# Causal attention on one core: half blocks of keys in 64 by 64 tiles, with loads and routing steps in other places

## The chip, the cores and the metric

The kernel runs on one core of one Trainium2 chip. A core has five engines with a queue each: TensorE (PE; its weight loads are listed apart as PEld) multiplies matrices into PSUM, VectorE (DVE), ScalarE (ACT) and GpSimd (POOL) work element by element, SyncE (SP) only starts transfers here. The metric is the device time of one execution in microseconds; less is better. Before the change the median of three runs is 746.33 us (744.14 to 746.45).

## The reference

Two layers follow each other. The first is a causal attention with a bias that lowers the weight of keys by what was summed up between key and query:

```python
scores = scale * np.matmul(q, k.transpose(0, 1, 3, 2))          # B, H, S, D = 8, 8, 576, 64
cum = np.cumsum(np.maximum(s, 0.0), axis=-1)
bias = -(cum[:, :, :, None] - cum[:, :, None, :])
scores = np.where(causal, -1e9, scores + np.minimum(bias, 0.0))
attn = exp(scores - max) / (sum + 1e-9)
x = matmul(attn, v)                                             # then (B, S, 512)
```

The second routes each of the 4608 tokens of 512 numbers to one of 8 experts, by the largest of 8 logits or, where a local gate says so, by the choice of the token ahead of it. Its output is `p[e] * (relu(x @ w1[e]) @ w2[e])` with 1024 hidden numbers. All is in float32.

## The kernel before, in words

**Work.** There are 32 pairs of heads (n = 0 to 31, `NPAIR`; 4 pairs make a batch). The two heads of a pair lie on partitions 0 to 63 and 64 to 127 of `qb` and `kb`. Scores are made with keys on the output's partitions: `scores(n, u)` (L893) makes one of four units of `UNITS` (L40), each up to 448 query columns wide, into a PSUM tile `ps` of two banks, one for each head. ACT takes the exponential into an SBUF tile `e` (L905), and POOL sets what lies above the diagonal to zero (`masked`, L889). A unit has blocks of 128 keys, and each block is multiplied by all queries from its first one on. Since a step of queries is 64 wide, half of the first 64 by 128 columns of a block is work for nothing. The bias is not added to the scores: it factors into a weight of the key, exp(cum minus a reference), that is multiplied into v (`weigh`, L876, into `vg`), and two columns beside v carry the weight and a one, so that the products hold the sums too.

`values(n, j0, j1)` (L924) forms the outputs of query blocks j of 64: 128 keys by 64 queries of `e` are the stationary operand, 66 columns of `vg` the moving one, and the results of the blocks add up in `po`. The blocks 0 to 5 have one PSUM bank (`po0`), the blocks 6 to 8 another (`po6`), and both are used by all pairs in turn. `evacuate` (L938) divides on DVE by the sum (a reciprocal and a product) and puts the result into `xb`. `turn` (L947) transposes it for the routing products.

**Order.** All engines run in the order in which the program is written (a schedule by hand). The loop at L1002 has 16 slots m, each with two pairs: the scores of both, then the values of both, then transposes and the weighing of later pairs (`WEIGHED`). Between these stand places, `at(m, 0)` to `at(m, 5)`, at which steps of routing and of the experts are put in (`plan`, L964): 0 and 1 behind the scores of the first and second pair, 3 and 4 behind the values of the first and second pair, 5 at the slot's end. A step's instructions stand on each engine in this order. A group of two batches is routed in steps: `product` (TensorE), `logits`, `codes`, `turn1`, `exps` (ACT), `turn2`, `ranks` (TensorE), `rows`, `gates` (mostly DVE), and then 18 `scatter` steps of POOL, which write rows of `xb` to a table in DRAM, placed by `STORES` (L49). In place 3, 4 and 5 a scatter first copies a number of `recs`, the reciprocal of the last values, so POOL waits there for DVE. `assign_early` (L411) chooses the experts of the first units; the expert stage (`Experts.run`, L649) then runs over units of up to 256 tokens.

**Loads.** SP starts them in order. `load_qk` (L790) and `load_v` (L802) take a buffer that an earlier pair has left; with `behind`, ACT first copies one number into the buffer, from a tile that is made at a chosen point, and this holds the load back until that point. In each slot, two v tiles go behind the second pair's unit 1, and the four tiles of q and k for the slot after the next behind the values of the first pair. PSUM has eight banks: `ps_s` holds three tiles of two banks that units, routing products and other short products use in turn (`banks`, L784), and `ps_o` the two of `po`.

## Time and profile before

| what | time |
|---|---|
| median of three runs | 746.33 us |
| the profiled execution | 748.85 us |
| its span, from the first instruction to the last | 747.1 us |
| attention, slots 1 to 15 (start of the first scores to the first expert product) | 19.85 to 221.63 us |
| TensorE busy | 729.2 us |
| exponentials of the scores on ACT, 128 of them | 97.0 us |
| masks on POOL, 160 of them | 67.2 us |
| scatters of rows to the table on POOL, 54 counted together | 54.5 us |

Times are of one profiled execution. "Busy" counts a stretch in which an instruction of the engine runs; matmuls overlap in a pipeline, so the mean time of one is not the pace at which they follow each other. A group's line gives source line, engine, operation, output and inputs, shapes and count, then busy time, mean time in ns, and the idle time ahead of it with what ended it. In the chain that ended last each piece is what the next one waited for; "issue" stands for time in which nothing that is recorded was waited for.

### The profile page before, as it was taken

Reading aid. Unit: us, or ns where it says so; the run is one execution under the profiler, and the core shown is the slowest. Engines: PE = TensorE matmul, PEld = TensorE weight load, DVE = VectorE, ACT = ScalarE, POOL = GpSimd, SP = SyncE. Lnnn points to the kernel's source line nnn. Section 1 sums busy time; section 2 is a strip of 40 time slices with the busy share of each in tenths; the row PEclk is TensorE's granted clock in tenths of the full one; section 3 lists DMA queues with packets and bytes.
Section 4 is the critical chain, followed back from the end, with each engine's and each line's share of the span. In section 5 each row is a group of like instructions: output and inputs, shape, how many; then the busy total and the mean of one; then the engine's idle time right before and its main releaser. Section 6 shows DMA issues by size and latency. Waiting matters only on the chain.

```text
span 747.1 us, 16231 instructions
## 1 busy us (share of the span) xinstructions
PE 729.2 (98%) x6537; PEld 504.9 (68%) x6537; DVE 257.7 (34%) x714; ACT 166.0 (22%) x355; POOL 206.7 (28%) x453
## 2 busy tenths in 40 slices
PE   8999999999998999999999999999999999999996
PEld 7888878878876567567567365637644676673675
DVE  4656668677756383101100411041132001104110
ACT  4645454354331011011011010201010111110111
POOL 3543367577574245350100011010101001000100
PEclk9999999999998999999999999999999999999999
DMA  8464455665629996598555979996999965976700
GB/s 303 145 189 149 152 191 165 201 199 172 188 81 382 341 396 218 208 424 240 203 190 169 375 258 396 342 382 237 425 334 390 423 215 214 307 268 239 269 15 32
DMA packets 57205, 187.28 MB, mean 251 GB/s; under 512 B 11837, under 2 KB 32061, under 8 KB 49568
## 3 DMA queue, kind: packets, MB, share of 16 engines
q1 hardware_dynamic: 50224, 165.91, 62.3%
q0 software_dynamic: 6800, 20.09, 7.0%
q8 instruction: 53, 0.87, 0.5%
q14 instruction: 32, 0.26, 0.1%
q10 hardware_dynamic: 96, 0.15, 0.1%
HBM read 165.50 MB, written 20.75 MB: 249 GB/s over the span
## 4 chain that ended last, share of the span: by engine, by line
PE 95%; issue 2%; POOL 1%; DVE 1%; DMA 1%; ACT 0%; SPq 0%; POOLq 0%; ACTq 0%
PE yp L637 34%; PE hp L608 31%; PE po L934 13%; PE ps L904 11%; PE hp L599 4%; PE lp L217 2%; DMA qb<-in_q_dram 1%; POOL table L349 0%; ACT e L905 0%; PE pos L301 0%; POOL e L890 0%; PE pos L302 0%; DVE xb L942 0%; SPq L799 0%; POOL out_dram L641 0%
## 5 line engine op out<-in xcount | busy, mean ns | idle before, releaser
L637 PE MATMUL yp<-w2b,hT 128*128 128x512 f32 (+4 forms) x768 | 258.4, 584 | 0.0
L608 PE MATMUL hp<-xT,w1b 128*128 128x256 f32 (+2 forms) x1216 | 232.0, 352 | 0.0
L608 PEld LDWEIGHTS hp<-xT,w1b 128*128 128x128 f32 x1216 | 207.7, 192 | 30.0 <-issue 7.8
L637 PEld LDWEIGHTS yp<-w2b,hT 128*128 128x128 f32 (+3 forms) x768 | 109.9, 167 | 138.4 <-issue 136.1
L641 POOL DMA_INDIRECT out_dram<-y,gi x37 | 36.4, 984 | 412.3 <-DVE y L639 380.0
L610 ACT ACTIVATE hT<-hp 128x256 f32<-128x256 f32 (+2 forms) x152 | 53.6, 353 | 430.4 <-PE hp L608 417.2
L639 DVE TENSOR_SCALAR y<-yp,gi 128x512 f32<-128x512 f32 (+2 forms) x38 | 27.8, 731 | 299.8 <-PE yp L637 293.4
L934 PE MATMUL po<-vg,e 128*64 128x66 f32 x3200 | 105.2, 223 | 6.9 <-issue 5.6
L934 PEld LDWEIGHTS po<-vg,e 128*64 128x64 f32 x3200 | 98.7, 138 | 13.1 <-issue 10.5
L905 ACT ACTIVATE e<-ps 128x768 f32<-128x768 f32 (+1 forms) x128 | 97.0, 837 | 46.5 <-PE ps L904 45.8
L904 PE MATMUL ps<-qb,kb 64*128 64x192 f32 (+4 forms) x768 | 94.7, 398 | 0.6 <-ACT e L905 0.3
L904 PEld LDWEIGHTS ps<-qb,kb 64*128 64x128 f32 x768 | 64.7, 186 | 29.6 <-ACT e L905 14.9
L890 POOL TENSOR_SCALAR_AFFINE_SELECT e<-e 128x256 f32<-128x256 f32 (+1 forms) x160 | 67.2, 444 | 50.3 <-ACT e L905 49.3
L349 POOL DMA_INDIRECT table<-xb,idx x54 | 54.5, 1009 | 19.6 <-issue 16.8
L619 DVE STREAM_TRANSPOSE hT<-hs 32x256 f32<-32x256 f32 x64 | 27.9, 436 | 78.9 <-ACT hs L601 78.1
L884 DVE TENSOR_TENSOR vg<-va,wk 128x256 f32<-128x256 f32 x64 | 41.5, 714 | 0.0
L941 DVE RECIPROCAL recs<-po 128x12 f32<-128x12 f32 x64 | 13.5, 211 | 64.0 <-PE po L934 45.2
L599 PE MATMUL hp<-w1b,xT 128*32 128x512 f32 (+1 forms) x224 | 28.3, 594 | 0.0
L578 DVE STREAM_TRANSPOSE xT<-xq 128x1024 f32<-128x1024 f32 (+1 forms) x23 | 23.6, 1028 | 11.8 <-DMA xq<-table 11.7
L942 DVE TENSOR_TENSOR xb<-po,recs 128x384 f32<-128x384 f32 (+1 forms) x48 | 22.0, 458 | 2.2 <-POOL xb L325 0.6
L599 PEld LDWEIGHTS hp<-w1b,xT 128*32 128x32 f32 (+1 forms) x224 | 8.1, 114 | 17.8 <-issue 17.8
L953 DVE STREAM_TRANSPOSE xt<-xb 128x576 f32<-128x576 f32 x24 | 17.1, 751 | 0.0
(254 smaller groups left out, 202.6 us busy)
## 6 DMA issues: line engine op xcount, KB each, us to landing
w2b<-in_w_dram SPq DMA_DIRECT2D x30, 2048.0 KB
w1b<-in_w_dram SPq DMA_DIRECT2D x29, 2048.0 KB
va<-in_v_dram SPq DMA_DIRECT2D x32, 320.0 KB
kb<-in_k_dram SPq DMA_DIRECT2D x31, 288.0 KB
qb<-in_q_dram SPq DMA_DIRECT2D x31, 288.0 KB
xq<-table SPq DMA_DIRECT2D x56, 130.0 KB
w1b<-in_w_dram SPq DMA_DIRECT2D x4, 512.0 KB
xq<-table SPq DMA_DIRECT2D x20, 65.0 KB
```

The lines of the kernel that those rows point to most:

```text
L349: put = self.nc.gpsimd.indirect_dma_start(out=self.halves, in_=src, element_offset=0, in_offset=None, out_offset=bass.IndirectOffsetOnAxis ...
L599: mm(ps[d, :], lhsT=xT[:, k, d], rhs=self.ws[l][0][:, k, c * 512 : c * 512 + 512], start=(k == 0), stop=(k == DK - 1))
L608: mm(ps[:, :w], lhsT=self.ws[ls[0]][0][:, k, c * P : c * P + P], rhs=xT[:, k, :w], start=(k == 0), stop=(k == DK - 1))
L610: nc.scalar.activation(self.hT[u][:, c, :w], ps[:, :w], Act.Relu)
L619: self.nc.vector.transpose(hT[32 * a : 32 * a + 32, :, 32 * r : 32 * r + 32], hs[32 * r : 32 * r + 32].rearrange("p (c i) -> p c i", i=P)[ ...
L637: mm(ps[d, :], lhsT=hT[:, k, n * P + d.start : n * P + d.stop], rhs=self.ws[l][1][:, k, f : f + w], start=(k == 0), stop=(k == FK - 1))
L641: put = nc.gpsimd.indirect_dma_start(out=self.out[:, :], out_offset=bass.IndirectOffsetOnAxis(ap=gi.bitcast(I32)[:m, n, 0:1], axis=0), in_ ...
L884: nc.vector.tensor_tensor(vg[:, to].rearrange("p c h e -> p (c h) e")[:, :, :DH], va[:, :c].rearrange("p c h e -> p (c h) e"), wk[:, n, to ...
L890: nc.gpsimd.affine_select(out=ap, in_=ap, compare_op=Alu.is_ge, fill=0.0, base=base, pattern=n, channel_multiplier=-1)
L904: mm(ps[:, h, at : at + z - a], lhsT=kb[d, key : key + P], rhs=qb[d, a:z], start=True, stop=True)
L905: nc.scalar.activation(e, ps, Act.Exp, scale=scale)
L934: mm(po[d, j - j0, :], lhsT=weights_of(n, c, j, h), rhs=vgs[n % NV][:, c if j < 2 * G1 else G1 + c, h, :], start=(c == 0), stop=(c == last))
```

## The change

The keys of a pair are stored in another order of blocks of 64: 8, 0, 1, 2, 3, 5, 4, 7, 6 (`BLOCKS`). Blocks 0 and 1, 2 and 3, 5 and 4, 7 and 6 form the tiles of 128 keys, and block 8 stands alone. A tile now is multiplied only by the queries from its second block in time on. The products of the query blocks 0, 2, 4 and 6 with their own keys are left out there. They are made apart, by `scores_halves`, in products of 64 keys by 64 queries over 64 rows, for both pairs of a slot into one PSUM tile, with one exponential and two masks, and kept in `eh`. `values_halves` multiplies them by v, again 64 by 64. Scores have three units in place of four (widths 512, 448, 384), and the values of a pair 21 steps per head in place of 25, with four half ones.

The order within a slot becomes: scores of both pairs; values of the first pair and its halves; halves of the second pair; half scores of the next slot; the first pair's two divisions; place 3; the values of the second pair, each part with its division; place 4. The second pair's sums lie in a tile of `ps_s`, the first pair's in `ps_o`, and the blocks are split 0 to 3 and 4 to 8.

Loads go out in three parts: two v tiles behind the first pair's unit 2, q and k of one pair behind the second pair's unit 1, q and k of the other behind the second pair's unit 2. At the start four v tiles are loaded in place of six, q and k of pair 3 ahead of v of pair 2, and q and k of pair 0 in other pieces. `logits`, `turn2`, `rows`, `gates` and `assign_early` move from place 3 to place 1, which is ahead of the divisions; the copies of `logits` run on ACT where a group has two batches. The exponentials of the key weights come one unit earlier.

The core of the diff:

```diff
-NJA = 6
+NJA = 4
-UNITS = (((0, 0, 384, 0),), ((0, 384, S, 0), (3, 384, S, 192)), ((1, P, S, 0),), ((2, 256, S, 0), (NF, TS, S, 320)))
-WIDTH = (384, 384, 448, 384)
+BLOCKS = (8, 0, 1, 2, 3, 5, 4, 7, 6)
+UNITS = (((0, DH, S, 0),), ((1, 3 * DH, S, DH), (NF, TS, S, 0)), ((2, 5 * DH, S, 0), (3, 7 * DH, S, 256)))
+WIDTH = (512, 448, 384)
+TURNED = (2, 3)
+ROOM = (512, 448, 512)
+HALVES = ((0, 4), (2, 6))
-FIRST = ((0, P, 0, 3 * P), (P, S, 3 * P, S))
+FIRST = 3 * P
...
+        copy = self.nc.scalar.copy if len(bs) == GB else v.tensor_copy
...
-                v.tensor_copy(l[32 * r : 32 * r + 32, b * NJ + j + skip : b * NJ + j + n],
-                              lt[32 * c : 32 * c + 32, skip:n, r, : E + 1])
+                copy(l[32 * r : 32 * r + 32, b * NJ + j + skip : b * NJ + j + n],
+                     lt[32 * c : 32 * c + 32, skip:n, r, : E + 1])
...
-        for k0, k1, q0, q1 in FIRST if n == 0 else ((0, S, 0, S),):
-            nc.sync.dma_start(kb[:, k0:k1], k[b][:, hp, k0:k1])
-            nc.sync.dma_start(qb[:, q0:q1], q[b][:, hp, q0:q1])
+        todo = [(kb, k, 0, S), (qb, q, 0, S)] if n else [(kb, k, 0, DH + P), (qb, q, 0, FIRST), (qb, q, FIRST, S), (kb, k, DH + P, S)]
+        for to, src, a, z in todo:
+            nc.sync.dma_start(to[:, a:z], src[b][:, hp, a:z])
...
+    load_qk(3)
     load_v(2)
-    load_qk(3)
-    for n in range(3, NVA):
-        load_v(n)
+    load_v(3)
...
         for i in range(G1 + NB):
-            d = slice(TL if i == G1 + NF else 0, P)
-            nc.vector.tensor_copy(wk[d, :, i, :].rearrange("p n h -> p h n"), cps[d, i].rearrange("p (h n) -> p h n", h=2))
+            d = slice(0, P)
+            c = i - G1
+            for to, of in (heads[:2],) if c == NF else (heads, heads[::-1]) if c in TURNED else ((d, d),):
+                nc.vector.tensor_copy(wk[to, :, i, :].rearrange("p n h -> p h n"),
+                                      cps[of, i].rearrange("p (h n) -> p h n", h=2))
...
+            key = 0 if c == NF else DH + c * P
+            for a, z, at in ((a, FIRST, at), (FIRST, z, at + FIRST - a)) if (n, u) == (0, 0) else ((a, z, at),):
+                for h, d in enumerate(heads):
+                    mm(ps[:, h, at : at + z - a], lhsT=kb[d, key : key + P], rhs=qb[d, a:z], start=True, stop=True)
+        nc.scalar.activation(e[:, :, : WIDTH[u]], ps, Act.Exp, scale=scale)
+        if u == 0:
+            masked(e[:, :, :DH], [[0, 2], [1, DH]], DH)
+        elif u == 1:
+            masked(e[:, :, :P], [[0, 2], [1, P]])
+        else:
+            masked(e[:DH].rearrange("p h (t i) -> p (h t) i", t=2)[:, :, :DH], [[0, 4], [1, DH]])
+
+    def scores_halves(m, ps):
+        if 2 * m >= NPAIR:
+            return
+        eh[m] = p_eh.tile([P, 2, 2, len(HALVES), DH], F32, name="eh")
+        ps = ps[:, :, : 4 * DH]
+        for i in range(2):
+            qb, kb = ins[2 * m + i]
+            for t, blocks in enumerate(HALVES):
+                for side, x in zip(heads, blocks):
+                    at = (2 * i + t) * DH
+                    key = BLOCKS.index(x) * DH
+                    for h, d in enumerate(heads):
+                        mm(ps[side, h, at : at + DH], lhsT=kb[d, key : key + DH], rhs=qb[d, x * DH : x * DH + DH],
+                           start=True, stop=True)
+        nc.scalar.activation(eh[m].rearrange("p h n t i -> p h (n t i)"), ps, Act.Exp, scale=scale)
+        by = eh[m].rearrange("p h n t i -> p (h n t) i")
+        masked(by[:DH], [[0, 8], [1, DH]])
+        masked(by, [[0, 8], [1, DH]], DH)
...
+    PARTS = ((0, NJA), (NJA, NJ))
+    def room(n):
+        if n % 2:
+            po = banks("pb")
+            po = [po[:, i] for i in range(2)]
+        else:
+            po = [ps_o.tile([P, 512], F32, name=f"po{i}") for i in range(2)]
...
+    def values(n, po, part, first, last):
+        a, z = PARTS[part]
+        steps = [(j, c) for j in range(a, z) for c in [*range((j + 1) // 2), *([NF] if j == NJ - 1 else [])]]
...
+    def values_halves(n, po, first):
+        e = eh[n // 2][:, :, n % 2]
+        for t, blocks in enumerate(HALVES):
+            for part, (side, j) in enumerate(zip(heads, blocks)):
+                for h, d in enumerate(heads):
+                    mm(po[part][d, j - PARTS[part][0], :], lhsT=e[side, h, t],
+                       rhs=vgs[n % NV][side, j // 2 + (G1 if part else 0), h, :],
+                       start=(first and t == 0), stop=(not first and t == 1))
...
-        plan(m, 3, lambda g=g: router.logits(g))
+        plan(m, 1, lambda g=g: router.logits(g))
...
-        plan(m + 1, 3, lambda g=g: router.turn2(g))
+        plan(m + 1, 1, lambda g=g: router.turn2(g))
...
-        plan(m + 2, 3, lambda g=g: router.rows(g))
-        plan(m + 2, 3, lambda g=g: router.gates(g, [xs[b] for b in range(g * GB, g * GB + GB)]))
+        plan(m + 2, 1, lambda g=g: router.rows(g))
+        plan(m + 2, 1, lambda g=g: router.gates(g, [xs[b] for b in range(g * GB, g * GB + GB)]))
...
-    plan(m - 5, 3, lambda: router.assign_early(0))
+    plan(m - 5, 1, lambda: router.assign_early(0))
...
-    plan(m - 1, 3, lambda: router.logits(NG - 1, (0,)))
+    plan(m - 1, 1, lambda: router.logits(NG - 1, (0,)))
...
+                if n > 1 and (n % 2, u) == (0, 2):
+                    load_v(n + NV, es[n][u][0:1, 0, DH : DH + 1])
+                    load_v(n + 1 + NV)
+                if n > 1 and (n % 2, u) == (1, 1):
+                    load_qk(n - 1 + NV, es[n][u][0:1, 0, P : P + 1])
             at(m, n - 2 * m)
...
+        a, b = pair
+        po = room(a)
+        for i in range(2):
+            values(a, po, i, True, False)
+        values_halves(a, po, False)
+        halves = banks("ph") if b + 1 < NPAIR else None
+        to = room(b)
+        values_halves(b, to, True)
+        scores_halves(m + 1, halves)
+        for n in pair if m == 0 else (b,):
+            load_qk(n + NV, es[b][2][0:1, 0, DH : DH + 1])
+        evacuate(a, po, 0)
+        evacuate(a, po, 1)
+        at(m, 3)
+        for i in range(2):
+            values(b, to, i, False, True)
+            evacuate(b, to, i)
+        at(m, 4)
```

What is left out stores k and v in the new order of blocks and reads them so in a path for inputs out of range, which is not run here.

## The prediction

> **What bounds the kernel now.** I read the page's busy line and chain first. They show TensorE in use almost throughout, with its matmuls making up the chain:
>
> ```profile
> PE 729.2 (98%) x6537; PEld 504.9 (68%) x6537; DVE 257.7 (34%) x714; ACT 166.0 (22%) x355; POOL 206.7 (28%) x453
> PE 95%; issue 2%; POOL 1%; DVE 1%; DMA 1%; ACT 0%; SPq 0%; POOLq 0%; ACTq 0%
> ```
>
> So an edit pays what it takes off TensorE's own stream in attention, which is the first 222 us; the expert stage behind it is not touched. Next, the chain in order of time (start, length, what), at quiet slots. A slot is two pairs of heads: their scores, then their values.
>
> ```profile
> 19.85 5.76 PE ps L904 x48
> 25.61 5.98 PE po L934 x200
> 31.59 5.76 PE ps L904 x48
> ...
> 61.15 2.31 PE lp L217 x64
> ```
>
> A quiet slot is 5.76 + 5.98 = 11.74 us with no pause. Third, the groups of TensorE matmuls kept apart by shape, for the tile sizes and counts (the mean in them is latency, not pace):
>
> ```profile
> L934 PE MATMUL po<-vg,e 128*64 128x66 f32 x3200 | 105.2, 223 | 6.9 <-issue 5.6
> L904 PE MATMUL ps<-qb,kb 64*128 64x448 f32 x128 | 29.6, 539 | 0.1
> L904 PE MATMUL ps<-qb,kb 64*128 64x384 f32 x128 | 28.7, 525 | 0.3 <-ACT e L905 0.3
> L904 PE MATMUL ps<-qb,kb 64*128 64x192 f32 x256 | 26.4, 325 | 0.2 <-DMA qb<-in_q_dram 0.2
> L904 PE MATMUL ps<-qb,kb 64*128 64x320 f32 x128 | 22.6, 430 | 0.0
> L904 PE MATMUL ps<-qb,kb 64*128 64x64 f32 x128 | 10.7, 244 | 0.0
> ```
>
> Each product appears as two instructions (3200 for 1600 value products), which I call passes. Starts of single instructions around 31.5 to 37.9 us give the pace: the two heads' passes start 6.5 ns apart and run together; the next two start after 323 ns at 384 columns, 376 at 448, 269 at 320, 162 at 192, 55 at 64, 58.3 at 66. That is 2.5 ns + columns/1.2. At a change of tile shape there is a hole: 202 ns instead of 55 from scores to values, then 108 instead of 58; 150 instead of 58 back, then 427 instead of 323. Each change costs about 197 ns. A 64-column score followed by a wider one costs about 112 ns more, because the next weights are not there yet.
>
> Fourth, the engines' busy time by slot (columns: length; then PE, PEld, DVE, ACT, POOL busy with counts; clock; DMA share; GB/s), and the chain inside a slot with scatters:
>
> ```profile
> 19.85:31.59 11.74, 11.74 (x250) 9.96 (x250) 6.39 (x14) 6.59 (x13) 6.52 (x25) 1.00 0.40 128
> 93.65:107.33 13.68, 12.73 (x250) 10.43 (x250) 7.75 (x20) 6.59 (x13) 8.94 (x20) 1.00 0.59 186
> 148.40:162.91 14.51, 13.14 (x250) 10.57 (x250) 9.83 (x35) 6.60 (x13) 9.94 (x22) 1.00 0.64 198
> ```
> ```profile
> 149.28 0.56 DVE xb L942
> ...
> 150.82 1.47 POOL table L349
> ...
> 153.67 1.13 POOL e L890 x3
> ...
> 154.84 1.96 PE po L934 x59
> ```
>
> Slots 1 to 15 run from 19.85 to 221.63 us, 201.8 us. Quiet pace would be 15 x 11.74 = 176.1, plus routing products 3 x 2.31 + 1.46 = 8.4 and ranks 3 x 0.72 = 2.2: 186.7. The other 15 us are pauses, nearly all in slots where POOL scatters rows: some follow the late DVE, POOL, mask chain above, more are clusters of two or three holes of about 0.4 us, put down to "issue", inside the values.
>
> **What the Trainium skill says.** "TensorEngine Tiling (Array Packing)", Key Properties: "Changing tiling mode (not just tile) drains the TensorE"; the trace agrees, with the 197 ns. The same page, Available Configurations, counts four independent 64x64 tiles; no run here shows one yet, but the routing product (128x32 tiles) runs four at once: 64 passes in 2.31 us. "TensorE: Matmul & The Clock Gate", Part 3, says row and column tiles compose; again not shown here. "Runtime: NRT & Kernel Launch", Instruction fetch mechanics, has each engine's instructions refilled in 16 KiB blocks of 256; the page's instruction queue moved 53 packets in 0.87 MB, which agrees, and makes fetching a candidate for the "issue" holes.
>
> **The change, part by part** (per pair of heads, then per slot).
>
> Scores: before, passes of 384, 192 twice, 448, 320, 64, each twice: 2 x (322.5 + 325 + 375.8 + 269.2 + 55.8) = 2.697 us. After: 512, 384, 64, 256, 128, each twice: 2 x (429.2 + 322.5 + 55.8 + 215.8 + 109.2) = 2.265. Per slot -0.86. Both 64-column products now stand in front of a wider one, before only one did: +0.11.
>
> Values: 25 steps become 21 (20 + 1 for the last block), two passes of 58.3 ns each: -0.466 per pair, -0.93 per slot.
>
> Halves: per pair 8 score products and 8 value products of 64x64. If four tiles run together, a pair takes 2 sets x 2 passes x 55.8 = 0.22 us of scores and 2 x 2 x 58.3 = 0.23 us of values; per slot +0.91. If only two run together, the double, +1.82. The trace of before shows two on rows and two or four on columns at once, so I take four; two is the other bound.
>
> Changes of tile shape: scores, values, halves, values, scores makes four instead of two: 2 x 0.197 = +0.39 (bounds 0.28 to 0.40, as the weights exposed are 64 or 128 columns wide).
>
> Sum per slot: -0.86 + 0.11 - 0.93 + 0.91 + 0.39 = -0.38 us, over 16 slots -6.1 us.
>
> ACT: 7 activations for 8, 2 x (1024 + 896 + 768) + 512 elements for 6400; it was busy 6.6 of 11.74 us and stays below TensorE. Twenty-seven logits copies of some 0.2 us go from DVE to ACT, where they stand behind the last exponentials and in front only of that slot's half scores and load releases, needed a slot later: nothing on ACT's side. Without that cover it would be 2 us in each of three slots.
>
> POOL: masks for 1152 elements x 4 instead of 5 instructions per pair; before 4 x 0.41 + 0.28 = 1.92 us. After 0.28 + 0.41 + 0.41 = 1.10 and, per slot, two of 512 elements (estimate 0.65 each from 0.28 at 128 and 0.41 at 256): 3.5 for 3.8 per slot, equal for our purpose. But a scatter row takes about 1.0 us and 0.4 around it, so five make 7 us: 10.5 us in a slot that shrinks to 11.36. Hidden still, with under 1 us to spare.
>
> DVE: rows and gates (11 + 2 instructions, 146.10 to 149.02 us in one slot: 2.9 us), turn2 (12, some 3.3 us) and assign_early (once, some 17 of 0.18: 3 us) go from behind the first pair's division to in front of it; gates' two iotas (0.3 us) move on POOL likewise, past two masks of half scores and a scatter. They then run under the first values (2.5 us). Behind them wait the divisions, and behind those POOL's gated scatters and then the next slot's masks. The second pair's sums get their own banks, the load's release no longer stands before a division (DVE waited 13.0 us, off the path mostly, for that copy). I put -2 us on the pauses, bounds -8 to +8: this is what the trace doesn't price.
>
> Loads: the same bytes, minus two value loads at the start (320 KB each) which move to slot 1: 4 value loads there, 1.28 MB, 6.4 us at the 200 GB/s seen, used some 9 us later: hidden. Keys and queries go out earlier, one pair at a time, rather than 1.15 MB at once behind the first values. SP's order stays filled with loads whose releases come in order; no load of the experts is put behind a later wait. This may thin the holes; it is inside the bounds above.
>
> Start: the first keys grow from 64 to 96 KB, two more copies of key weights (0.17 each) precede the weighing that the first values need; ACT's chain there loses one activation: +0.3. Half scores of slot 0 fit under that ACT-bound stretch.
>
> Sum: -6.1 - 2 + 0.3 = -7.8 on the profiled execution's 748.85 us (span 747.1, 1.75 around it), 741. It was 2.5 us above the median of the runs; the median goes from 746.33 to about 738.5. I round to 739.
>
> **The rivals.** (1) The helper engines become the bound: in the seven slots with five or more scatters POOL's 10.5 us, DVE's 10 and the waits between them hold the masks past the scores, now 1 us shorter. It decides once 0.87 us is lost in each of these slots (7 x 0.87 = 6.1). For: slots of 93.65 and 148.40 have POOL at 9 to 10 us. Against: in these slots POOL still waited for DVE or ACT. It gives 743 to 750. (2) Slower: the four 64x64 tiles do not run together but two by two, because the row halves block each other or the passes of one product come back to back. Then +0.91 more per slot, a slot is 0.53 us longer, +8.5 us: 753 with the -2. It decides from 0.42 of that doubling. For: no such tile in the trace. Against: row tiles pair, column tiles pair and quadruple. (3) The pauses mostly vanish, as loads are spread and banks are doubled: 8 of 15 us more or less gone, 6.1 + 7 = 13: 730 to 734.
>
> **How the numbers follow.** Likeliest (734 to 743): 0.55. Rival 1: 0.20, of which 0.05 under, 0.11 within and 0.04 over. Rival 2: 0.13. Rival 3: 0.12. Under 0.3% (2.2 us, about what a measurement of this kernel can tell from no change) fall 0.55 + 0.12 + 0.05 = 0.72; within, 0.11; slower, 0.04 + 0.13 = 0.17. The range 730 to 752 leaves out half of rival 3 and most of rival 2's upper half, under 0.2; faster holds most of the chance, the likeliest own range is 734 to 743.
>
> **What would show it.** Quiet slots of about 11.35 us; half products as sixteen passes per pair and kind in 0.23 us, four starts 6.5 ns apart; four holes of 0.15 to 0.2 us per slot; first values near 12.8 us; slot 1's start near 19.5. Wrong if quiet slots are 11.7 or more (rival 2 shows as starts by twos), if masks appear as TensorE's releaser in scatter slots (rival 1), or if the 3.3 us of holes in the routing product at 228 to 231 us, as the expert weights start to load, grow or go away: they are placed by what the loads and the fetching do, and can move the sum by 3 us.

## The result, and the profile after

The changed kernel took 747.39 us in the median of eight runs (745.73 to 749.9); the kernel before, in eight runs too, 744.45 (743.99 to 747.22). The ratio is 1.0036, with a 95% interval of 1.0016 to 1.0056: slower by 0.36%, where 1% faster was forecast. The profiled execution took 745.73 us (span 744.0), the fastest of the eight, while the profile of before that the prediction worked from had been an execution of 748.85 us, slower than all eight of before. So the two first pages can't be subtracted, and each kernel was profiled again, on chip 0. The chip of the first pair is not on record. On chips 0, 3 and 11, where all the experiments ran, the kernel before is 2% quicker (729.4 to 729.9 us), and the ratio, timed on chip 11, is 1.0036 again (1.0022 to 1.0051).

The page's busy line and the chain of the kernel after, which answer to the first two lines shown of before:

```profile
PE 720.3 (97%) x6925; PEld 494.4 (66%) x6925; DVE 247.3 (33%) x689; ACT 167.9 (23%) x381; POOL 202.6 (27%) x421
PE 94%; issue 2%; ACT 1%; POOL 1%; DMA 1%; DVE 0%; SPq 0%; POOLq 0%; ACTq 0%; DVEq 0%
```

TensorE is busy 9 us less (the forecast took 6.1 us off its stream), but it issues 6925 passes for 6537. The chain in order of time (start, length, what) at the first slots:

```profile
32.44 4.96 PE ps L915 x40
37.40 2.60 PE po L974 x84
40.00 0.39 PE po L986 x16
40.39 0.23 PE pb L986 x16
40.62 0.47 PE ph L937 x32
41.09 2.01 PE pb L974 x62
43.10 0.68 issue
43.78 0.86 PE pb L974 x21
44.64 4.96 PE ps L915 x40
```

Scores 4.96, first values 2.60, the halves 0.39 + 0.23 + 0.47, second values 2.60: a quiet slot is 11.25 us for 11.74 before, and the forecast was 11.36. But there is a hole, put down to "issue", inside the second values. Slots 1 to 3 of before lose 0.3 us in all. TensorE's passes by shape during attention (busy us, mean ns, then idle time before them and its releaser):

```profile
L974 PE MATMUL pb<-vg,e 128*64 128x66 f32 x1344 | 44.9, 224 | 5.2 <-issue 5.2
L974 PE MATMUL po<-vg,e 128*64 128x66 f32 x1344 | 44.1, 224 | 1.2 <-issue 1.2
...
L915 PE MATMUL ps<-qb,kb 64*128 64x384 f32 x128 | 26.5, 491 | 2.4 <-ACT e L916 1.7 <-DMA kb<-in_k_dram 0.4 <-issue 0.2
...
L937 PE MATMUL ph<-qb,kb 64*64 64x64 f32 x512 | 12.0, 221 | 1.6 <-issue 1.6
...
L986 PE MATMUL pb<-vg,eh 64*64 64x66 f32 x256 | 7.7, 219 | 1.0 <-issue 1.0
```

Most of the idle time stands in front of the second pair's values (pb), the ones behind the halves. By slot (columns: length; then PE, PEld, DVE, ACT, POOL busy with counts; clock; DMA share; GB/s):

```profile
19.84:32.44 12.60, 11.57 (x274) 9.42 (x274) 6.08 (x14) 6.50 (x14) 5.44 (x17) 1.00 0.82 264
32.44:44.64 12.20, 11.53 (x274) 9.50 (x274) 8.73 (x18) 6.33 (x12) 8.06 (x26) 1.00 0.50 158
...
161.31:177.67 16.36, 14.60 (x338) 11.71 (x338) 9.26 (x19) 8.46 (x20) 11.13 (x20) 1.00 0.65 210
```

From here on the pause of a slot is its length less the quiet 11.25 us (11.74 before) and less the 2.31, 0.72 or 1.46 us of routing work in it. Pauses, unlike times, are always those of one profiled execution. In this pair of profiles slots 1 to 15 of after have 20.7 us of pauses, those of before 15.2.

### The profile page after: what moved, and what is told of

Same layout as the page of the kernel before. It is cut to its first block, busy times and chain, and to the rows that moved or that the text cites. A ratio compares the mean times of both kernels' runs of the same rounds, so it can differ in the third digit from the quotient of the medians.

```text
span 744.0 us, 16963 instructions
## 1 busy us (share of the span) xinstructions
PE 720.3 (97%) x6925; PEld 494.4 (66%) x6925; DVE 247.3 (33%) x689; ACT 167.9 (23%) x381; POOL 202.6 (27%) x421
## 4 chain that ended last, share of the span: by engine, by line
PE 94%; issue 2%; ACT 1%; POOL 1%; DMA 1%; DVE 0%; SPq 0%; POOLq 0%; ACTq 0%; DVEq 0%
PE yp L642 34%; PE hp L613 31%; PE ps L915 9%; PE po L974 6%; PE pb L974 6%; PE hp L604 4%; PE lp L221 2%; ACT e L916 1%; PE ph L937 1%; PE po L986 1%; PE pb L986 1%; DMA kb<-in_k_dram 1%; POOL table L354 0%; DVE wk L871 0%; PE pos L306 0%
## 5 line engine op out<-in xcount | busy, mean ns | idle before, releaser
L916 ACT ACTIVATE e<-ps 128x1024 f32<-128x1024 f32 (+2 forms) x96 | 82.8, 909 | 44.9 <-PE ps L915 39.8
L915 PE MATMUL ps<-qb,kb 64*128 64x64 f32 (+5 forms) x644 | 83.3, 405 | 3.9 <-ACT e L916 3.1
L915 PEld LDWEIGHTS ps<-qb,kb 64*128 64x128 f32 x644 | 53.0, 187 | 32.2 <-ACT e L916 10.9
L899 POOL TENSOR_SCALAR_AFFINE_SELECT e<-e 128x128 f32<-128x128 f32 (+2 forms) x96 | 40.7, 433 | 38.7 <-ACT e L916 37.8
L974 PE MATMUL pb<-vg,e 128*64 128x66 f32 x1344 | 44.9, 224 | 5.2 <-issue 5.2
L974 PEld LDWEIGHTS pb<-vg,e 128*64 128x64 f32 x1344 | 41.6, 138 | 7.3 <-issue 6.1
L974 PE MATMUL po<-vg,e 128*64 128x66 f32 x1344 | 44.1, 224 | 1.2 <-issue 1.2
L974 PEld LDWEIGHTS po<-vg,e 128*64 128x64 f32 x1344 | 41.3, 138 | 4.3 <-issue 2.0
L892 DVE TENSOR_TENSOR vg<-va,wk 128x256 f32<-128x256 f32 x64 | 37.7, 654 | 0.0
L899 POOL TENSOR_SCALAR_AFFINE_SELECT eh<-eh 64x512 f32<-64x512 f32 (+1 forms) x32 | 20.9, 654 | 42.3 <-ACT kb L803 38.0
```

What stands on the lines that cost most here:

```text
L892: nc.vector.tensor_tensor(vg[:, to].rearrange("p c h e -> p (c h) e")[:, :, :DH], va[:, :c].rearrange("p c h e -> p (c h) e"), wk[:, n, to ...
L899: nc.gpsimd.affine_select(out=ap, in_=ap, compare_op=Alu.is_ge, fill=0.0, base=base, pattern=n, channel_multiplier=-1)
L915: mm(ps[:, h, at : at + z - a], lhsT=kb[d, key : key + P], rhs=qb[d, a:z], start=True, stop=True)
L916: nc.scalar.activation(e[:, :, : WIDTH[u]], ps, Act.Exp, scale=scale)
L974: of = mm(po[part][d, j - a, :], lhsT=weights_of(n, c, j, h), rhs=vgs[n % NV][:, c if j < 2 * G1 else G1 + c, h, :], start=(first and i == ...
```

## The experiments

They ran on chip 0 (before_again, after_again, moves_back, loads_back), chip 3 (shift, noload, mix, spread) and chip 11 (after_timed, before_loads, mixv, combo). Each ratio is to runs of the kernel before on the same chip, with medians of 729.40, 729.52 and 729.87 us. before_again, after_again, shift and noload are single executions. Three theories stood at the start. **A**: the moved steps put DVE, ACT and POOL work in front of the divisions. **B**: the loads let go in three parts collide with the fetching of TensorE's instructions. **C**: the scatters hold up a chain of scores and exponentials whose slack the wider units took away. Theory D came out of the first runs.

### Both kernels again, one part undone at a time

before_again and after_again have no edit.

> The kernel before, unchanged, for a second profile: its first profiled execution (span 747.1 us) was slower than every timed one. All theories expect about 744.5 us, slots 1 to 15 from 19.85 to about 219 us with some 12 us of pauses; what is shorter than in the first profile tells where an execution's scatter lies.

> The changed kernel, unchanged, for a second profile: its first profiled execution (745.73 us) was the fastest of eight. Expected 747.4 us, quiet slots of 11.25 us again, and slots 1 to 15 with 21 to 24 us of pauses against 15 before. If the pauses are no longer than before, the loss lies behind attention.

Measured: 729.45 us (span 727.7) and 732.01 (730.3). Slot 1 starts at 19.44 and 20.06 us, attention ends at 208.38 and 210.87, and what lies behind it takes 519.4 us in both (519.35 and 519.43). So the whole loss is in attention: start +0.62, fifteen slots x (11.25 - 11.74) = -7.35, pauses 2.29 before and 11.51 after, +9.22; sum +2.49 of the 2.6 us between the spans. The chain of before_again, then of after_timed (the changed kernel once more, below):

```profile
69.18 5.76 PE ps L904 x48
74.94 5.98 PE po L934 x200
80.93 5.76 PE ps L904 x48
```
```profile
69.88 4.96 PE ps L915 x40
74.84 2.60 PE po L974 x84
77.44 0.39 PE po L986 x16
77.83 0.23 PE pb L986 x16
78.07 0.47 PE ph L937 x32
78.53 2.36 PE pb L974 x74
80.89 1.39 issue
82.28 0.56 PE pb L974 x10
```

Before: no pause at all. After: the gain of half a microsecond is there, and 1.39 us are lost ten passes before the end of the second values. The first miss is in my reading of before: its 12 to 15 us of pauses, expected here too, were 2.3.

moves_back undoes the moves (six plans go from place 1 back to place 3) and the copies on ACT:

```diff
-        copy = self.nc.scalar.copy if len(bs) == GB else v.tensor_copy
+        copy = v.tensor_copy
-        plan(m, 1, lambda g=g: router.logits(g))
+        plan(m, 3, lambda g=g: router.logits(g))
...
```

> The changed kernel with one part undone: logits, turn2, rows, gates and assign_early go back behind the first pair's division, and the logits copies back to DVE. Theory A (the moved steps put DVE, ACT and POOL work in front of the divisions, and the pauses come from there): 743 us or less, 3.5 us or more gained on the changed kernel, the pauses of the slots from 93 us on gone down. Theory B (the loads let go in three parts collide with the fetching of TensorE's instructions) and theory C (the scatters hold up a chain of scores and exponentials whose slack the wider units took away): no change, 746 to 749 us.

Measured: 734.9 us, 1.0079 of before (1.0051 to 1.0108). Worse than the change, not better: theory A is out. The moved steps seem worth some 0.4%, 3 us (1.0079 against 1.0036, on two chips; the intervals touch at 1.0051). The profiles agree: 14.2 us of pauses for 11.5, and four waits of scores for DVE's transposes, 1.5 us, which after_again has not.

loads_back undoes the loads:

```diff
-                if n > 1 and (n % 2, u) == (0, 2):
-                    load_v(n + NV, es[n][u][0:1, 0, DH : DH + 1])
-                    load_v(n + 1 + NV)
-                if n > 1 and (n % 2, u) == (1, 1):
-                    load_qk(n - 1 + NV, es[n][u][0:1, 0, P : P + 1])
+                if (n % 2, u) == (1, 1):
+                    load_v(n - 1 + NVA, es[n][u][0:1, 0, P : P + 1])
+                    load_v(n + NVA)
...
+        load_qk(a + NV, po[1][0:1, 0, 0:1])
+        load_qk(b + NV)
```

> The changed kernel with one part undone: keys and queries of two pairs let go together behind the first pair's values, values by twos at the second pair's second unit, six value loads at the start, all as in the kernel before. Theory B (the new order of the loads makes the holes inside the values, by delaying TensorE's instructions): holes of slots 1, 2, 5 and 6 (1.03, 0.67, 0.36, 0.51 us in the first profile after) gone, 742 to 744 us. Theories A and C: the holes stay, 746 to 749 us.

Measured: 730.14 us, 1.0019 (1.0007 to 1.003; this overlaps the changed kernel's 1.0022 to 1.0051). Pauses fall from 11.5 to 8.0 us, but slot 1 starts at 21.51. The holes of slots 1 and 2 shrink (0.74 and 0.61 us for after_again's 1.63 and 1.69), that of slot 3 all but goes (0.2 for 1.49), those of slots 5 and 6 do not shrink (0.53 and 0.73 for 0.45 and 0.39), and two later ones grow (before passes 2887 and 3141, 1.46 and 1.89 for 0.36 and 0.74): theory B is half right.

What these traces have in common gave theory D. Holes stand in front of the same passes in all three profiles of the changed kernel: 600, 853, 1745, 1998, 2633, 3141, 3775 and a few more. Counted over all of TensorE's instructions (weight loads, passes, waits), these are numbers 1218, 1729, 3522, 4033, 5314, 6338 and 7617: each 193 or 194 past a multiple of 256, which I call a block border. The Trainium skill, "Runtime: NRT & Kernel Launch", Instruction fetch mechanics, says an engine's instructions are refilled in 16 KiB blocks of 256 and that crossing a boundary is mostly hidden. The block size agrees: the page of after has

```profile
q8 instruction: 56, 0.92, 0.5%
```

56 packets of 16 KB on the instruction queue (columns: packets, MB, share). "Mostly hidden" does not hold for the holes shown here. With the packets' times beside the blocks (block by instruction number; when it was begun and used up; how long after its beginning the packet started, the packet's length, and the time from its landing to the next block's first instruction):

```
before_again  1217-1473  38.06-41.82  used 3.76   packet +1.57, took 0.96, then 1.22
before_again  1729-1985  50.01-53.85  used 3.85   packet +0.78, took 1.56, then 1.50
after_again    961-1217  27.91-32.83  used 4.91   packet +2.07, took 1.46, then 1.38
after_again   1473-1729  40.65-45.35  used 4.70   packet +2.31, took 0.95, then 1.43
after_again   1985-2241  53.02-57.66  used 4.64   packet +2.18, took 0.97, then 1.49
after_again   2497-2753  65.48-69.27  used 3.79   packet +0.61, took 1.01, then 2.18
```

A block was never begun earlier than 1.1 us after the last packet had landed, and after a hole mostly 1.2 to 1.6. Most packets take 0.9 to 1.1 us. A block that lies wholly in the values of the kernel before is used in 3.7 us without a hole, so by estimate the next packet may start up to 3.7 - 0.95 - 1.4 = 1.35 us after its beginning. In the changed kernel the halves put 64 passes with their 64 weight loads, half a block, into 0.39 + 0.23 + 0.47 = 1.09 us; a block around them is used in 3.1 us, and the next packet may start only 0.75 us after its beginning. What it is later than that becomes a hole. Blocks mostly of scores take over 6 us and do not wait. This is theory D: **a hole needs a dense block and a late packet.** The next table takes the dense blocks of slots 1 to 15, those with at most 40 instructions of scores among the 256 (16 of them with the old tiles, 18 with the new): how long after the block's beginning the packet started, in the median and at the latest; the shortest use of a block; and the holes of 0.2 us or more at block borders, number and sum (a hole is the time from one pass's start to the next less the usual 0.055 us; the profile's views, which work with modelled ends, count less).

```
              chip  packet starts after   shortest use   holes at borders
before_again    0     0.46 (to 1.95)         3.56           1   0.2
after_again     0     1.24 (to 2.41)         3.05          13  10.1
after_timed    11     1.23 (to 2.46)         3.05          13   9.0
moves_back      0     1.44 (to 3.32)         3.05          11  10.0
loads_back      0     0.68 (to 2.59)         2.95           9   6.9
before_loads   11     0.47 (to 2.37)         3.56           1   0.8
mix             3     0.58 (to 2.26)         3.06           8   5.4
mixv           11     0.74 (to 1.73)         2.90           5   2.2
noload          3     0.31 (to 2.44)         2.90           1   1.5
combo          11     0.65 (to 1.50)         3.30           2   0.7
```

So the changed kernel has both: packets 0.8 us later, for which mostly its release of the loads answers (0.68 in loads_back), and blocks 0.5 us shorter. The first pair of profiles agrees: one hole of 0.25 us at a border before, seven with 6.3 us after, while all other pauses stay at 14 to 15 us. (Runs not yet named follow below.) The medians depend by up to 0.2 us on which blocks are counted as dense.

### Theory D put to the test

shift moves every instruction of TensorE on by half a block and changes nothing else:

```diff
-    warm_up(8)
+    warm_up(40)
```

> The changed kernel with 40 warm-up products of TensorE in front of everything for 8: 64 passes more, so every later instruction of TensorE stands half a block of 256 further on; nothing else changes. Theory D (a hole arises where TensorE reaches a multiple of about 127.5 passes, that is of 256 instructions, before the packet with its next instructions has landed): the holes of slots 1 to 3 and 5 to 7, which stood before passes 600, 853, 1108, 1745 and 1998 in every profile of the changed kernel, leave those places of the program (now numbered 664, 917, 1172, 1809, 2062) and stand before 600, 728, 855 and the like by the new count wherever that falls into values or halves; the sum of pauses stays at 8 to 14 us. Theories A and C: they stay at the same places of the program, that is at 664, 917, 1172.

Measured: 734.57 us; the longer warm-up puts slot 1's start 7 us later, at 27.14. No hole in the values or halves stays at its place of the program. They stand before passes 600, 1490, 1745, 1998, 2887, 3522 and 3775 of the new count, that is 64 passes earlier in the program, and all at instruction numbers 193 or 194 past a multiple of 256; two that stood in the second values are now in the half scores (1998 and 2887), and those of 853 and 1108 are gone. Pauses 7.05 us, just under what was expected. Which instruction stands at the border does not matter, the count does: this is shown.

noload takes the late packets away: loads of pairs 8 to 31 are left out.

```diff
+        if n >= 8:
+            ins[n] = ins[n - 4]
+            return
...
+        if n >= 8:
+            vs[n] = kept[n % NVA if n % NVA > 1 else n % NVA + 6]
+            return
```

> The changed kernel without the loads of keys, queries and values for pairs 8 to 31: the tiles of earlier pairs are used again, so these loads are left out and the rest of the work is the same. Theory D: instruction packets find free queues, start within 1.2 us and take 0.95; a block that holds the halves is used in about 3.1 us, so holes of slots 5 to 10 shrink to 0.3 us or less each and the pauses of slots 4 to 10 (3 to 4 us in the second profile after) to under 1.5 us. Theory that the stream alone is too dense, whatever the loads do: holes of 0.4 to 0.7 us stay at passes 1745 and 1998.

Measured: attention ends at 200.87 us, 7.5 before the kernel before, with pauses of 2.02 us, 1.62 of them in slot 1, where loads still ran. (With foreign keys the sums fall outside the range that the kernel tests for, and it takes its slow path behind attention, 2187.59 us in all; only attention is read.) By slot, the three slots from 68.71 us on, then the same three of after_timed:

```profile
68.71:79.96 11.25, 11.25 (x276) 9.38 (x272) 9.52 (x35) 5.97 (x10) 3.53 (x8) 1.00 0.01 3
79.96:91.93 11.97, 11.97 (x280) 9.93 (x276) 8.83 (x26) 5.77 (x9) 4.41 (x10) 1.00 0.02 4
91.93:103.18 11.25, 11.25 (x276) 9.37 (x272) 6.08 (x14) 5.87 (x10) 7.43 (x16) 1.00 0.11 38
```
```profile
69.88:82.84 12.96, 11.57 (x274) 9.56 (x274) 9.55 (x35) 6.44 (x13) 3.55 (x8) 1.00 0.56 180
82.84:95.53 12.69, 12.18 (x278) 10.01 (x278) 8.83 (x26) 6.22 (x12) 4.32 (x10) 1.00 0.44 133
95.53:107.47 11.94, 11.47 (x275) 9.51 (x274) 6.08 (x14) 6.33 (x13) 8.27 (x16) 1.00 0.57 187
```

With 3 GB/s on the queues for 180 the slots are 11.25 us to the digit (11.97 with 0.72 of ranks). Two dense blocks, in the columns used above:

```
noload        3777-4033  87.86-90.97   used 3.11   packet +0.19, took 1.02, then 1.89
noload        4289-4545  98.59-101.70  used 3.11   packet +0.16, took 1.09, then 1.86
```

So the stream alone is not too dense; it is so with loads on the queues. (With the loads ACT's release copies go too, but they could not tie the holes to a count of TensorE's instructions, as shift does.) And the forecast of the stream was right: all of 7.35 us appears as soon as the loads are gone.

before_loads is meant as the other half, the late packets without the new dense blocks: the kernel before with the changed kernel's loads, but for the last keys and queries of a slot, which still wait for the first pair's values.

```diff
-                if (n % 2, u) == (1, 1):
-                    load_v(n - 1 + NVA, es[n][u][0:1, 0, 0:1])
-                    load_v(n + NVA)
+                if n > 1 and (n % 2, u) == (0, 2):
+                    load_v(n + NV, es[n][u][0:1, 0, P : P + 1])
+                    load_v(n + 1 + NV)
+                if n > 1 and (n % 2, u) == (1, 1):
+                    load_qk(n - 1 + NV, es[n][u][0:1, 0, P : P + 1])
...
```

> The kernel before with one part of the change alone: its loads in the changed kernel's order (four value loads at the start, the loads of a slot let go in three parts). Its densest block of 256 instructions of TensorE lies wholly in the values and is used in about 3.7 us. Theory D (a hole needs both a late packet and a dense block): packets come as late as in the changed kernel, but pauses of slots 1 to 8 grow by 2 us at most from the 0.5 us of the second profile before; 0.999 to 1.003 of before. Theory that the new order of loads costs by itself: pauses of 8 us or more, 1.010 or more of before.

Measured: 731.87 us, 1.0032 (1.0021 to 1.0043), pauses 4.79 us, no hole of 0.2 us or more at a border in slots 1 to 10. What it does cost is 0.22 us in nearly every slot, in the scores. The chain of before_loads:

```profile
43.32 5.98 PE ps L903 x48
49.30 5.98 PE po L933 x200
```

Scores of 5.98 us for 5.76. The view of groups puts 18.0 us of the weight loads' idle time in the scores down to ACT's exponentials (15.0 in before_again): ACT has one load release more (a copy of some 0.2 us) between them. That the copy is the cause is argued only. In the median the packets came no later here than in before_again (0.47 and 0.46 us), a miss: I had expected them as late as in the changed kernel (1.23). Why much the same order of loads delays packets there and not here isn't settled; the two differ in the length of a slot and in what the last keys and queries wait for.

One packet did come late, and it made a hole. The block of instructions 6081 to 6337 lies wholly in the values of slot 11. Its successor's packet started 2.37 us after it was begun, landed at 157.08 us, and the next instruction, number 6338, started at 158.53: 1.45 us after the landing, with a hole of some 0.8 us, at a border. The block was used in 4.70 us for 3.68. (The profile puts this wait down to a load of keys issued at 155.04, but that one is for slot 13; the keys of slot 12 had been issued at 138.65 and landed by 142.17.) So the old values have fetch holes too when a packet is late beyond the 1.35 us estimated above; the changed kernel's blocks need less lateness for it. What this run doesn't show is how the kernel before fares with packets as late as the changed kernel's throughout.

after_timed is the changed kernel, timed beside these:

> The changed kernel, unchanged, timed in the same call as the three others, so that their ratios can be set against its own. All theories: 1.002 to 1.006 of before; fetch holes before passes 600, 853, 1108, 1745 and 1998 again, pauses of slots 1 to 15 of 10 to 13 us.

Measured: 732.95 us, 1.0036 (1.0022 to 1.0051), pauses 10.09 us, of which holes over 0.15 us make 9.2. All but one of 0.18 us stand 193 or 194 past a multiple of 256, and none waits for an exponential. In this profile theory C has at most 1 us to explain.

### Versions that keep the gain

mix takes the changed kernel's start and the old release in the slots (the value loads that the start no longer makes go behind the second pair's second unit in slot 0 and the first pair's first unit in slot 1):

```diff
+                if (n % 2, u) == (1, 1):
+                    load_v(n - 1 + NVA if n > 1 else 4, es[n][u][0:1, 0, P : P + 1])
+                    load_v(n + NVA if n > 1 else 5)
...
+        load_qk(a + NV, po[1][0:1, 0, 0:1])
+        load_qk(b + NV)
```

> The changed kernel with fewer loads at the start as it has them, but in the slots keys and queries of two pairs let go together behind the first pair's values and values by twos, as before. Putting the whole release back gave 1.0019 of before with slot 1 starting 1.5 us later than in the changed kernel. If that late start came from the loads at the start alone, this gives 1.0019 - 0.0020 = 0.9995 to 1.000 of before, slot 1 at 20.1 us, pauses of slots 1 to 15 near 8 us. If the release in the slots is what costs the start, 1.002 to 1.003.

Measured: 728.21 us, 0.9988 (0.9975 to 1.0002), slot 1 at 19.47, pauses 6.31. The fewer loads at the start are worth having (loads_back, which has not got them, has 1.0007 to 1.003 and slot 1 at 21.51); the release in three parts is not.

spread pulls the dense stretch apart. It also lets the last keys and queries of a slot go behind the first pair's values, not behind the second pair's unit 2:

```diff
-        for i in range(2):
-            values(a, po, i, True, False)
-        values_halves(a, po, False)
...
+        values_halves(a, po, True)
         values_halves(b, to, True)
-        scores_halves(m + 1, halves)
+        for i in range(2):
+            values(a, po, i, False, True)
...
+        if b + 1 < NPAIR:
+            scores_halves(m + 1, banks("ph"))
```

> The changed kernel with its dense stretch pulled apart: the value halves of both pairs run first, then the first pair's values, then the second's, then the half scores of the next slot; the same products and as many changes of tile shape. Before, 64 half passes stood together between the values, and a block of 128 passes around them was used in about 3.1 us; now the densest block takes 3.6 (32 half passes in 0.46 us, a change of shape 0.2, 96 value passes of 31 ns). Theory D: each hole gets some 0.5 us shorter, 4 to 6 us in all: 0.995 to 0.998 of before. Theories A and C: nothing gained, and the half scores' exponential now stands in front of the next slot's first one: 1.003 to 1.008 of before.

Measured: 733.51 us, 1.0044 (1.0028 to 1.006): a miss on the time. The holes at borders fell to 5.7 us from after_timed's 9.0, but the sum of the slots' pauses only to 9.57 from 10.09, because waits for POOL's masks came in (2.4 us in three), and slot 1 started at 23.59 us for 20.06. The chain at the start shows why: in slot 0 the first values now stand behind the half scores' exponential and its masks.

```profile
13.70 0.50 ACT eh L939
14.19 0.06 issue
14.25 0.66 POOL eh L899
14.91 0.06 issue
14.97 0.67 POOL eh L899
15.68 0.46 PE po L986 x16
```

mixv is mix with the value loads let go at the first pair's second unit, 2.5 us earlier in the slot:

```diff
-                if (n % 2, u) == (1, 1):
+                if n > 1 and (n % 2, u) == (0, 1):
...
```

> The variant with fewer loads at the start and the release in the slots as before (0.9988), with one move: the value loads are let go at the first pair's second unit instead of the second pair's, 2.5 us earlier, so that less of them still runs when the packets for the dense blocks are asked for, at the start of the values. Theory D: holes before 600, 853, 2251, 2633, 2887 and 3141 shorter by 1 to 3 us in all, 0.995 to 0.998 of before. If loads hold up packets only in the second half of a slot: no change, 0.9985 to 1.0.

Measured: 724.33 us, 0.9922 (0.9901 to 0.9943), pauses 3.34 us: faster than both kernels, from the place of one release, and by more than forecast. The second values of the slot shown above for after_timed now run without a hole:

```profile
68.89 4.96 PE ps L915 x40
...
77.55 2.60 PE pb L974 x84
80.15 4.96 PE ps L915 x40
```

The loads now run more in the scores, where a block of instructions lasts about 7 us: in the first microsecond of the dense blocks other transfers keep the 16 DMA engines busy for a share of 0.71 in after_timed, 0.55 in mix and 0.33 here. The median packet is no earlier than in mix (0.74 us for 0.58), but the latest ones are (before passes 2887 and 3141 0.24 and 0.82 us for 1.91 and 2.26). The two profiled executions differ by 2.0 us (724.04 and 726.08): 3.2 us less of holes at borders, and a start of slot 1 that is 1.0 us later. The ratios differ by more, 0.7%, and for that the profiles show no reason.

combo is mixv with spread from slot 1 on, and POOL's constants of slot 1 moved from place 5 to place 3.

```diff
+        if m:
+            values_halves(a, po, True)
+            values_halves(b, to, True)
+        for i in range(2):
+            values(a, po, i, m == 0, m > 0)
...
-    plan(1, 5, router.constants)
+    plan(1, 3, router.constants)
```

> The same with the dense stretch pulled apart too (from slot 1 on value halves first, half scores last; slot 0 keeps its order, which cost 3.5 us at the start when it was changed; POOL's constants of slot 1 one place earlier, since the next slot's masks waited 1.4 us for them). Theory D: fetch holes of 2 to 3 us in all instead of 6, with up to 1.5 us of waits for masks in slots with scatters against it: 0.992 to 0.996 of before. If the masks of the half scores, now at the slot's start, hold up POOL more than that: 0.998 or more.

Measured: 723.2 us, 0.9912 (0.9889 to 0.9935), just better than forecast; attention ending at 201.65 us, with pauses of 2.48. Its chain, its view of what TensorE waited for in slots 1 to 15 (us in total, times, longest), and the main line of the same view of after_timed:

```profile
67.51 4.96 PE ps L915 x40
72.47 0.39 PE po L986 x16
72.86 0.23 PE pb L986 x16
73.10 2.60 PE po L974 x84
75.70 2.45 PE pb L974 x84
78.15 0.62 PE ph L937 x32
78.77 4.96 PE ps L915 x40
```
```profile
PE pb L974 <- POOL e L899: 0.8, 1, 0.8
PE po L974 <- POOL e L899: 0.6, 1, 0.6
PE po L974 <- issue: 0.3, 2, 0.2
```
```profile
PE pb L974 <- issue: 6.7, 12, 1.4
```

The slot lasts 11.26 us without a hole, and the "issue" waits of after_timed's values are all but gone. What is left is two waits for masks in slots with scatters and two short holes. Against mixv no difference can be told: the intervals overlap.

## Why the prediction was wrong

**TensorE's stream: right.** Forecast -0.38 us per slot, measured -0.49: halves of 0.39 and 0.23 us of values and 0.47 of scores, changes of shape included, so four 64x64 tiles do run together; in after_timed at 77.89 us four passes start within 20 ns and the next four 56 ns after the first. Rival 2 (two by two) is out. Noload shows the whole of it, 7.5 us at the end of attention.

**The pauses: the step that failed.** "I put -2 us on the pauses, bounds -8 to +8: this is what the trace doesn't price", and of the loads "This may thin the holes; it is inside the bounds above". They did not shrink by 2 but grew: by 5.6 us in the first pair of profiles and by 9.2 us, beyond the bound, from before_again to after_again (by 7.8 to after_timed, on another chip). What grew is holes at block borders, 0.25 to 6.3 us in the first pair and 0.2 to 10.1 in the second. Between the second profiles that is more than the 7.4 us that the stream gained, and the sign turned. Two things were missed, both readable from the trace of before. Fetching was named as a candidate for the holes and then not counted: 388 passes more in 16 slots, each with its weight load, so 48 instructions more per slot, and half a block within 1.09 us, between values that already took four instructions every 58 ns. And the kernel before was close to the edge: in its first profile packets for the blocks in the values of slots 1 to 4 landed 1.82, 1.40, 1.87 and 2.47 us before their use, and the 1.40 came with the 0.31 us pause of slot 2, whose hole stands before instruction 1473, 193 past a multiple of 256. The shorter a block is used, the less lateness of its packet it can bear; with the loads on the queues, what the shorter stream gained went into holes.

**The pauses of before: over-read.** I took the 15 us for a property of the kernel. Nearly all of them, 14.9 us, are not at block borders, and they stand in both profiles of the first pair (14.4 in after, though it was the fastest of its eight). On chip 0 before_again has 2.3 us, so rival 3 (730 to 734, pauses vanishing) had nothing to win there. The holes in the routing product at 228 to 231 us were 2.5 us idle by the chain; 3.3 us is the whole stretch.

**The loads: wrong sign.** They were to thin the holes. Let go in three parts they delay the packets of the dense blocks: 1.24 us in the median, 0.68 with the old release. With the release in the slots as before, the change would have made no difference that can be told (mix, 0.9988, with 1 inside its interval), and with one release moved it is 0.8% faster (mixv).

**The moved steps: right in sign, as far as can be told.** They were put with the pauses at -2; undone, the kernel lost some 0.4%, 3 us, with intervals that touch.

**POOL and rival 1.** In the first pair part of it is there: 2.5 us in four waits of TensorE for an exponential in slots with scatters, where the view of waits of before has none. In after_again and after_timed there is no such wait. As all pauses that are not at borders stay at 14 to 15 us in the first pair, it didn't decide. That the median of 747.39 us fell into this rival's 743 to 750, and into the whole range of 730 to 752, is luck: another mechanism made the difference.

**Start.** Forecast +0.3; measured nothing in the first pair of profiles (19.84 for 19.85), +0.6 in the second and +0.8 in after_timed (20.24 us).

**The products of routing behind attention** (228 to 231 us): 519.4 us behind attention in both kernels on chip 0; no part in it.

What stays open: in the first pair both kernels show further holes in slots with scatters, by twos and threes of 0.5 us, at numbers that are no multiples of 256 apart, and the changed one the late exponentials just named. The later profiles show neither, so no run could take them apart, nor say why the first pair is 2% slower. Open too is what delays single packets: after_timed has one that started 1.66 us late with the queues busy for a share of 0.2.

## What to carry to other kernels

Where an engine's stretch is made of many short instructions, count instructions per microsecond beside busy time: here 256 of them in 3.1 us were often not fetched in time with loads on the queues, in 3.7 us they mostly were. Look for holes whose instruction numbers lie a fixed block apart; if they do, let the loads go so that they run under the stretches of long instructions, or mix long and short. And take a profile's pauses for a gain only after a second execution has shown them.

## What the hardware showed that was not expected

- Instruction packets are held up while data is loaded: in dense blocks they start 0.31 us after the block is begun (median of noload, with few loads), 1.23 us with the changed kernel's loads, up to 2.5 (3.3 in moves_back).
- From the last landing of a packet to the first instruction of the next block it never took less than 1.1 us in attention, in fourteen profiles.
- Four 64x64 tiles of fp32 run together: 16 passes of 66 columns in 0.23 us, as many in 0.39 with the change of shape in front.
- The same program took 744.45 us in the first runs and 729.4 to 729.9 on chips 0, 3 and 11, and the ratio of the two kernels was 1.0036 both in the first runs and on chip 11. Which chip the first was is not on record. In the two profiles of before 12.9 of the 19.4 us between the spans are pauses in attention.
